# Loads issued earlier, product P1 of the next superblock moved ahead of P3, and the attention's small matmuls put on column tiles

## The chip, the cores and the metric

The kernel runs on one core of a Trainium2 chip. The metric is the device time of one execution in microseconds (us), less being better. TensorE is called PE here as in the profile, VectorE DVE, ScalarE ACT, GpSimd POOL, and SyncE SP; SP issues every DMA of this kernel, in program order.

## The reference

Linear attention with a norm, then two two-layer perceptrons, all float32 (the weights arrive as float64):

```python
kv = np.einsum('bhsd,bhse->bhde', k, v)          # 8 batches, 8 heads, 576 tokens, 64 wide
out = np.einsum('bhsd,bhde->bhse', q, kv)
rms = np.sqrt(np.mean(out * out, axis=-1, keepdims=True) + 1e-06)
x = out / rms * g_norm                           # as 4608 tokens x 512
h = x @ w_in;  x = np.maximum(0.01 * h, h) @ w_out     # 512 -> 2048 -> 512
h = x @ w_in2; x = (h - np.tanh(h)) @ w_out2           # 512 -> 2048 -> 512
```

## The kernel before

**Arithmetic.** Each big product is cut into 2x2 blocks and done with seven block products instead of eight; P1 to P7 are these products (table `PROD`), and `Blocks` adds them up into the four blocks "11", "12", "21", "22". Each float32 operand is split into a high and a low float16 part (`hi` on ACT, `lo` on DVE), and three float16 matmuls make one product (`three`, L489). An operand's splits come as a tile `opa` (for P1, P2, P4) and a tile `ops` (for P3, P5, P6, P7).

**Passes.** There are four in a row: up 1 (`up`, moving operand 288 wide, eight superblocks of eight channel pairs, with the attention of the later batches in between), down 1 (`down`, eight superblocks of two halves t), up 2 and down 2 (256 wide, nine superblocks). An up pass writes its result `g` to DRAM, the next down pass reads it back (`gl`), down 1 writes `x` from tiles `xst`, up 2 reads it as `x1g`. Beside the passes the weights of the next passes are converted from float64 (`convert`: load `words`, ACT L314, four DVE steps, store `wf`) and split (`split_late`: load `unit<-wf`, ACT L362, DVE L365, POOL L372, store `wd`), then loaded into place (`w<-wd`).

**A down superblock.** PE does P1, P2, P4, P6, P7, P5, P3, each over all eight channel pairs j and for both halves. P3 adds on top of P5 in the same PSUM bank `ps_c`, so PE may start P3 of a half only when DVE has read block "22" out of it (`add`, L542). `produce` loads and splits the eight `gl` of the next superblock in the meantime.

**Attention.** For each pair of heads (`pair`): `kv` multiplies k and v of both heads in six float32 matmuls of 128 columns by 128 and uses the two diagonal 64x64 blocks (`kvd`); `qtr` transposes q, `o` multiplies (tile `po`), ACT squares, and `m` sums the squares of each head into row 8r+2c of a 16-row tile `pm`, in one matmul for each half r. In the trace each float32 matmul is two records (two passes). After four pairs, `norms` takes root and inverse (`iv`), stores it, and loads it back spread over the partitions (`bc`, L867), and POOL scales `xg` with it (L874); ACT and DVE then split `xg` (L429, L436).

**Order.** The order on every engine is fixed at build time by `Plan`: each step gets a planned time from the numbers written in the code (`plan.pe` counts PE's time, `chain` places a list of steps on engines A, V and G with their planned durations), and instructions are recorded in that order. A step such as `(None, 4.5, load)` puts the load 4.5 planned us ahead of its first use. At run time engines go through their queues in order and wait on semaphores. Slots L, M and X are buffers handed out by the planner.

Of the kernel before, what the change touches and what calls it, by code (L numbers as in the profile page):

```python
# [130 lines left out]
def body(ctx, tc, q, k, v, g_norm, w1, w2, w3, w4, out):  # L131
# [11 lines left out]
    NU = 4 * P  # L143
    NL, NM, NX = 20, 11, 13

# [23 lines left out]

    ivd = [scratch([2 * H, T1], F32, f"iv_{b}") for b in range(B)]  # L170
    x1d = {(c, s): scratch([P, 2 * T1], F32, f"x1_{c}_{s}") for c in range(DM // P) for s in range(NS1)}
# [20 lines left out]
    mw = const.tile([P, 4, 2 * NP], F32, name="mw")  # L192
    sel = const.tile([P, 4 * H - 2], F32, name="sel")
    kvd = [const.tile([P, P], F32, name=f"kvd{n}") for n in range(2)]

    def constants():
        for h in range(2):
            nc.sync.dma_start(out=gcol[D * h:D * h + D, :], in_=g_norm.rearrange("(p o) -> p o", o=1))
        make_identity(nc, ident)
        nc.vector.memset(ones, 1.0)  # L200
        nc.vector.memset(eps_sb, EPS / (X_SCALE * X_SCALE))
        nc.vector.memset(sel, 0.0)
        for n in range(2):
            nc.vector.memset(sel[D * n:D * n + D, 2 * H - 2 + n:2 * H - 1 + n], 1.0 / D)
            nc.vector.memset(kvd[n], 0.0)
        nc.vector.tensor_reduce(out=gabs, in_=gcol, axis=AX.X, op=ALU.max, apply_absolute_value=True)
# [175 lines left out]
    def split_late(n, i, kk, t, place):  # L382
# [256 lines left out]


    def down(blk, T, NS, mats, width, place, ready, start_of, freed, scales=None, scale=None):

# [32 lines left out]

        def superblock(s):
            t0 = plan.pe
            start_of(s, t0)
            if s + 1 < NS:
                produce(s + 1, t0 + 1.0)  # L680
            dur = mm(width)
            for t in range(2):
                sc = scales(s) if scales else (None, None)
                bk[s, t] = Blocks(
                    dict(a=t, b=2 + 3 * t, c=3 + 3 * t, d=4 + 3 * t), width, place(s, t), None, None, ready(s, t)
                )
                bk[s, t].now = {}
                if scales:
                    def late(s=s, t=t):
                        bk[s, t].scale, bk[s, t].minus = scales(s)  # L690
                    at(t0, late)

            def whole(p, t, js=range(NP)):
# [7 lines left out]
            late = range(len(early), NP)  # L701
            for p in (1, 2):
                for t in range(2):
                    if early:
                        whole(p, t, early)
            for p in (1, 2):
                for t in range(2):
                    whole(p, t, late)
            for j in range(NP):
                for t in range(2):  # L710
                    e = whole(4, t, [j])
                give("A", j, e)
            for p in (6, 7):
                for t in range(2):
                    whole(p, t)
            for t in range(2):
                whole(5, t)
            for t in range(2):
                e = whole(3, t, range(2))
            for j in range(2):  # L720
                give("S", j, e)
                if s == NS - 1:
                    freed(j, e)
            for j in range(2, NP):
                for t in range(2):
                    e = whole(3, t, [j])
                give("S", j, e)
                if s == NS - 1:
                    freed(j, e)

# [13 lines left out]
    PAIRS = (0, 2, 1, 3)  # L744
    D_KV, D_Q, D_O, D_M = 1.6, 0.7, 0.6, 0.55

    def load_pair(b, c, held):
        for nm, src in (("k", k), ("v", v), ("q", q)):
            held[nm] = L.take([CP, NC, 2, D], F32, nm)
            for h in range(2):  # L750
                nc.sync.dma_start(
                    out=held[nm].ap[:, :, h], in_=src[b, 2 * c + h].rearrange("(p c) d -> p c d", p=CP)
                )
# [6 lines left out]
    def pair(b, c, held):  # L760
# [4 lines left out]
        def kv():  # L765
            held["pk"], held["bank"] = att_bank("pk")
            for a in range(NC):
                nc.tensor.matmul(
                    out=held["pk"][:, :P], lhsT=two_heads(held["k"], a), rhs=two_heads(held["v"], a),
                    start=(a == 0), stop=(a == NC - 1),  # L770
                )

        def kv_after(e):
            def go():
                held["kvd"] = kvd[kv_n[0] % 2]
                kv_n[0] += 1
                for h in range(2):
                    r = slice(D * h, D * h + D)
                    nc.scalar.activation(out=held["kvd"][r, r], in_=held["pk"][r, r], func=AF.Copy)
                used.discard(held["bank"])  # L780
# [39 lines left out]

        def m(r):
            first, last = (c == PAIRS[0] and r == 0), (c == PAIRS[-1] and r == 1)
            if first:
                pm[b] = bank(5, "pm")
            row = H * r + 2 * c
            nc.tensor.matmul(
                out=pm[b][:2 * H, :T1], lhsT=sel[:, 2 * H - 2 - row:4 * H - 2 - row], rhs=sq[r].ap,
                start=first, stop=last,
            )
            X.give(sq[r])  # L830

        def m_after(r, e):
            if c == PAIRS[-1] and r == 1:
                norms(b, e)
# [3 lines left out]
            (D_Q, lambda: qtr(1), lambda e: q_after(1, e)), (D_O, lambda: o(0), lambda e: o_after(0, e)),  # L838
            (D_O, lambda: o(1), lambda e: o_after(1, e)), (D_M, lambda: m(0), lambda e: m_after(0, e)),
            (D_M, lambda: m(1), lambda e: m_after(1, e)),  # L840
        ]

    def norms(b, e):
        held = {}

        def root():
            held["iv"] = X.take([2 * H, T1], F32, "iv")
            nc.scalar.activation(
                out=held["iv"].ap, in_=pm[b][:2 * H, :T1], func=AF.Sqrt,
                bias=eps_sb[:2 * H], scale=1.0 / (X_SCALE * X_SCALE),  # L850
            )
# [10 lines left out]
        def load(kk):  # L862
            held[kk] = L.take([P, 4, T1], F32, "bc")
            rows = ivd[b].rearrange("(r h) t -> h r t", r=2)
            for n in range(2):
# [73 lines left out]
    def split_all():  # L939
        for n, (i, kk) in enumerate(UNITS):  # L940
            what = ("w", 0, i - 2, 1) if i >= 2 else "s_w1"
            when(what, plan.now + 0.3 + 2.5 * n, lambda i=i, kk=kk: plan.chain(plan.now, split_first(i, kk)))

    scaled[0] = [split_all]

    def early_pair(b, c, t, held):
        gaps = (0.0, 1.7, 2.5, 3.4, 4.4, 5.2, 6.2)
        for (dur, fn, after), g_ in zip(pair(b, c, held), gaps):
# [61 lines left out]

    spread(lambda i, kk, t: convert(1, i, kk, t, 6.0), UNITS, START + 52.0, START + 180.0)
    spread(lambda i, kk, t: split_late(1, i, kk, t, M), UNITS, START + 200.0, end1 - 60.0)
    spread(lambda i, kk, t: convert(2, i, kk, t, 6.0), UNITS, START + 182.0, end1 - 60.0)

# [80 lines left out]
    def x1_operands(s, t):  # L1095

        x1ops[s] = [{}, {}]
        for kk in range(2):
# [64 lines left out]
    c3 = end2 + 0.45 * (end3 - end2)  # L1163
    spread(lambda i, kk, t: convert(3, i, kk, t, 6.0), UNITS, end2 - 45.0, c3)
    e = c3 + 18.0
    scaled[3] = [lambda: [down_scales(state[x]) for x in ("whole", "rest")]]
    spread(lambda i, kk, t: split_late(3, i, kk, t, M), UNITS, e + 1.0, end3 - 55.0)


# [71 lines left out]
```

## Time and profile before

| | |
|---|---|
| median of 3 runs | 1646.12 us (1645.23 to 1646.91) |
| profiled execution | 1649.15 us, of which the span from first to last instruction is 1647.4 us |
| PE busy | 1512.3 us, 92% |
| DVE, ACT, POOL busy | 79%, 53%, 45% |
| granted PE clock, mean | 0.959 |

The profile is of one execution. The stages can be told apart in it: preparation and the first attention to 105 us, up 1 to 602, down 1 to 942, up 2 to 1309, down 2 to the end. A matmul's end is modelled and overlaps the next one's start, so what PE has done is read from start to start.

### The profile page before, as it was taken

How to read it: one execution, taken by the hardware profiler on the slowest of the kernel's cores; microseconds unless marked ns; L12 is line 12 of the kernel's file. 1: busy time of each engine (PE TensorE's matmuls, PEld its weight loads, DVE VectorE, ACT ScalarE, POOL GpSimd, SP SyncE). 2: the span in 40 equal slices, each digit the busy share in tenths (PEclk: the TensorE clock that was granted, in tenths of full speed). 3: DMA queues.
4: the chain of work that ended last, by engine and by line, in shares of the span. 5: the costliest groups of instructions: out<-in, count | busy, mean ns of one | idle time of the engine just before them, and what ended most of it. 6: DMA issues, size and time to landing. Idle time of an engine off the chain costs nothing. (4 is left out here: it accounts for less than half of the span.)

```text
span 1647.4 us, 32120 instructions
## 1 busy us (share of the span) xinstructions
PE 1512.3 (92%) x12274; PEld 1227.4 (75%) x12274; DVE 1301.6 (79%) x2113; ACT 867.2 (53%) x1381; POOL 746.0 (45%) x758
## 2 busy tenths in 40 slices
PE   5299898898989999999999979999999889999998
PEld 3156675666767777777777768888888778888887
DVE  4765676576667778889989669999999988888881
ACT  3366454465655664444444246666776645455441
POOL 0356203144143345666656134446887654444440
PEclk8589999999999999999999989999999999999999
DMA  9856897898896885545455565555666844444441
GB/s 210 172 88 160 227 239 208 245 245 235 252 259 209 282 318 168 185 145 200 155 172 173 184 233 206 186 210 196 243 240 243 316 143 143 157 129 135 145 132 33
DMA packets 251578, 322.08 MB, mean 196 GB/s; under 512 B 129440, under 2 KB 194080, under 8 KB 251424
## 3 DMA queue, kind: packets, MB, share of 16 engines
q1 hardware_dynamic: 251424, 320.03, 62.7%
q8 instruction: 96, 1.57, 0.4%
q14 instruction: 58, 0.48, 0.1%
HBM read 190.84 MB, written 129.12 MB: 194 GB/s over the span
## 5 line engine op out<-in xcount | busy, mean ns | idle before, releaser
L489 PEld LDWEIGHTS <-w 128*128 128x128 f16 x8400 | 824.8, 99 | 280.1 <-issue 98.7
L468 POOL TENSOR_TENSOR gl<-gl 128x256 f32<-128x256 f32 (+1 forms) x272 | 309.5, 1138 | 307.2 <-issue 79.9
L489 PE MATMUL ps_c<-ops,w 128*128 128x288 f16 (+1 forms) x2400 | 337.3, 285 | 40.2 <-DVE g L536 28.2
L489 PE MATMUL ps_a<-ops,w 128*128 128x288 f16 (+1 forms) x2400 | 333.6, 284 | 22.2 <-ACT u L527 10.3
L489 PEld LDWEIGHTS <-ops 128*128 128x128 f16 x1728 | 169.8, 98 | 28.8 <-issue 7.7
L372 POOL TENSOR_TENSOR unit<-unit 128x128 f32<-128x128 f32 x192 | 134.1, 699 | 116.0 <-DVE wo L365 97.4
L489 PE MATMUL ps_b<-opa,w 128*128 128x288 f16 (+1 forms) x1200 | 170.2, 287 | 0.0
L489 PE MATMUL ps_a<-opa,w 128*128 128x288 f16 (+1 forms) x1200 | 166.8, 283 | 2.9 <-DMA w<-wd 2.8
L489 PE MATMUL ps_d<-opa,w 128*128 128x288 f16 (+1 forms) x1200 | 165.9, 282 | 2.7 <-DVE g L536 2.7
L468 DVE TENSOR_TENSOR gl<-gl 128x256 f32<-128x256 f32 (+1 forms) x272 | 156.0, 576 | 3.3
L874 POOL TENSOR_TENSOR xg<-xg,bc 128x1152 f32<-128x1152 f32 x16 | 43.1, 2694 | 254.3 <-DMA bc<-iv 208.7
L1145 POOL TENSOR_TENSOR g<-g,th 128x512 f32<-128x512 f32 x72 | 101.0, 1403 | 95.9 <-ACT th L1142 95.7
L431 ACT ACTIVATE ops<-gl,inv 128x1024 f16<-128x1024 f32 x72 | 82.6, 1147 | 110.2 <-POOL gl L468 102.9
L489 PEld LDWEIGHTS <-opa 128*128 128x128 f16 x1296 | 126.8, 98 | 16.6 <-issue 1.9
L429 ACT ACTIVATE ops<-gl 128x1152 f16<-128x1152 f32 x64 | 74.3, 1162 | 99.5 <-POOL gl L468 94.6
L438 DVE SCALAR_TENSOR_TENSOR ops<-gl,inv,ops 128x1024 f16<-128x1024 f32 x72 | 104.4, 1451 | 15.8 <-ACT ops L431 15.4
L436 DVE TENSOR_TENSOR ops<-gl,ops 128x1152 f16<-128x1152 f32 x64 | 99.8, 1559 | 19.9 <-ACT ops L429 19.7
L365 DVE SCALAR_TENSOR_TENSOR wo<-unit,s_w,wo 128x384 f16<-128x384 f32 (+1 forms) x96 | 83.4, 871 | 27.1 <-ACT wo L362 26.7
L489 PE MATMUL ps_c<-w,ops 128*128 128x256 f16 x864 | 98.4, 275 | 3.8 <-DVE osb L536 3.8
L489 PE MATMUL ps_a<-w,ops 128*128 128x256 f16 x864 | 96.1, 273 | 3.2 <-ACT u L527 3.2
L468 POOL TENSOR_TENSOR x1g<-x1g 128x256 f32<-128x256 f32 x72 | 68.1, 946 | 65.1 <-DMA x1g<-x 34.7
L438 DVE SCALAR_TENSOR_TENSOR opa<-gl,inv,opa 128x768 f16<-128x768 f32 x72 | 87.2, 1211 | 12.5 <-ACT opa L431 12.5
(118 smaller groups left out, 2192.3 us busy)
## 6 DMA issues: line engine op xcount, KB each, us to landing
g<-g SPq DMA_DIRECT2D x64, 576.0 KB, 4.4
gl<-g SPq DMA_DIRECT2D x64, 576.0 KB, 4.7
g<-g SPq DMA_DIRECT2D x72, 512.0 KB, 3.0
gl<-g SPq DMA_DIRECT2D x72, 512.0 KB, 4.5
wd<-wo SPq DMA_DIRECT2D x48, 448.0 KB, 2.8
w<-wd SPq DMA_DIRECT2D x24, 896.0 KB, 7.4
words<-in_moe_w_in_dram SPq DMA_DIRECT2D x64, 256.0 KB, 5.0
words<-in_moe_w_out_dram SPq DMA_DIRECT2D x64, 256.0 KB, 4.0
```

The costliest lines, as they stand in the source:

```text
L365: nc.vector.scalar_tensor_tensor(out=dst()[:, 1, a:b], in0=cols(0, n), scalar=scale(), in1=dst()[:, 0, a:b], op0=ALU.mult, op1=ALU.subtract,)
L372: nc.gpsimd.tensor_tensor(out=o, in0=a, in1=b, op=ALU.subtract)
L429: nc.scalar.activation(out=o, in_=i_, func=AF.Copy)
L431: nc.scalar.activation(out=o, in_=i_, func=AF.Identity, scale=scale())
L436: nc.vector.tensor_tensor(out=o, in0=i_, in1=h, op=ALU.subtract)
L438: nc.vector.scalar_tensor_tensor(out=o, in0=i_, scalar=scale(), in1=h, op0=ALU.mult, op1=ALU.subtract)
L468: lambda: e.tensor_tensor(out=g()[:, o], in0=g()[:, a], in1=g()[:, b], op=op),
L489: nc.tensor.matmul(out=out_, lhsT=a, rhs=c, start=start and m == 0, stop=stop and m == n - 1, skip_group_check=not fresh,)
L874: nc.gpsimd.tensor_tensor(out=x, in0=x, in1=held[kk].ap, op=ALU.mult)
L1145: e.tensor_tensor(out=g()[:, n], in0=g()[:, n], in1=held["t"].ap[:, n], op=ALU.subtract)
```

## The change

- Leads of loads: `words` 6 to 13 planned us, `unit` 4.5 to 9, `bc` 5 to 6, `x1g` 5 to 10 with the whole chain begun 13 us earlier (15 for the first), q, k and v of later batches 13 instead of 9 places ahead. Slots: L 20 to 22, X 13 to 8.
- `down`: P1 of superblock s+1 is done between P5 and P3 of superblock s, pair by pair; P2 and P4 alternate pair by pair. `produce` starts 6.8 planned us before P2 (`AHEAD`), where it started 1 us after the start of P1.
- `kv`: each head gets matmuls of its own, 64 columns by 64, in two column tiles of PE's array (`tile_position` (0, 0) and (0, 64)); k and v lie with each head's rows together, so a DMA row is 384 elements instead of six times 64. `m`: one 32-column tile for each half, both halves issued together. `iv` has 64 rows instead of 16.
- Planned PE durations of a pair: 1.6, 0.7, 0.7, 0.6, 0.6, 0.55, 0.55 become 0.9, 0.5, 0.5, 0.6, 0.6, 0.7. The first weights are split unit pair by unit pair.

```diff
-    NL, NM, NX = 20, 11, 13
+    Q = 32
+    NL, NM, NX = 22, 11, 8
...
-        plan.chain(t, [(None, 4.5, load), (None, 0.0, room)] + stages + [(None, 0.0, store)])
+        plan.chain(t, [(None, 9.0, load), (None, 0.0, room)] + stages + [(None, 0.0, store)])
...
+    AHEAD = 6.8
...
-            if s + 1 < NS:
-                produce(s + 1, t0 + 1.0)
...
-            early = range(NP - 2) if s == 0 else range(0)
...
+            def in_turn(ps, s=s, then=None):
+                for j in range(NP):
+                    for p in ps:
+                        for t in range(2):
+                            e = whole(p, t, [j], s)
+                    if then:
+                        then(j, e)
+
+            start_of(s, plan.pe)
+            if s == 0:
+                blocks(0)
+                for js in (range(NP - 2), range(NP - 2, NP)):
+                    for p in (1, 2):
+                        for t in range(2):
+                            whole(p, t, js)
+            if s + 1 < NS:
+                produce(s + 1, plan.pe - AHEAD - (one if s == 0 else 0.0))
+            in_turn((4,) if s == 0 else (2, 4), then=lambda j, e: give("A", j, e))
+            for p in (6, 7, 5):
                 for t in range(2):
                     whole(p, t)
+            if s + 1 < NS:
+                blocks(s + 1)
+                in_turn((1,), s + 1)
...
+            in_turn((3,), then=end)
...
-    D_KV, D_Q, D_O, D_M = 1.6, 0.7, 0.6, 0.55
+    D_KV, D_Q, D_O, D_M = 0.9, 0.5, 0.6, 0.7
...
+            apart = nm != "q"
+            held[nm] = L.take([CP, 2, NC, D] if apart else [CP, NC, 2, D], F32, nm)
...
-                nc.tensor.matmul(
-                    out=held["pk"][:, :P], lhsT=two_heads(held["k"], a), rhs=two_heads(held["v"], a),
-                    start=(a == 0), stop=(a == NC - 1),
-                )
+                for h in range(2):
+                    nc.tensor.matmul(
+                        out=held["pk"][D * h:D * h + D, :D], lhsT=held["k"].ap[:, h, a], rhs=held["v"].ap[:, h, a],
+                        start=(a == 0), stop=(a == NC - 1), tile_position=(0, D * h), skip_group_check=True,
+                    )
...
+            for r in range(2):
+                nc.tensor.matmul(
+                    out=pm[b][Q * r:Q * r + Q, :T1], lhsT=sel[:, Q - 2 - 2 * c:2 * Q - 2 - 2 * c], rhs=sq[r].ap,
+                    start=first, stop=last, tile_position=(0, Q * r), skip_group_check=True,
+                )
+                X.give(sq[r])
...
-            more.append([(None, 5.0, lambda kk=kk: load(kk)), ("G", 2.7, lambda kk=kk: scale(kk))] + stages)
+            more.append([(None, 6.0, lambda kk=kk: load(kk)), ("G", 2.7, lambda kk=kk: scale(kk))] + stages)
...
-    OFFS = (1, 4, 6, 8, 10, 12, 14)
+    OFFS = (1, 4, 6, 8, 10, 13)
...
-            loads.append((n0 - 9, b, c, held))
+            loads.append((n0 - 13, b, c, held))
...
-    spread(lambda i, kk, t: convert(1, i, kk, t, 6.0), UNITS, START + 52.0, START + 180.0)
+    spread(lambda i, kk, t: convert(1, i, kk, t, 13.0), UNITS, START + 45.0, START + 173.0)
...
-            plan.chain(t + 3.5 * kk, [(None, 5.0, load)] + stages)
+            plan.chain(t + 3.5 * kk, [(None, 10.0, load)] + stages)
...
-            state["whole"] = second_scales(0, whole, t0 + 9.0)
-            x1_operands(0, t0 + 17.0)
+            state["whole"] = second_scales(0, whole, t0 + 5.0)
+            x1_operands(0, t0 + 2.0)
...
-            x1_operands(n // (NOP * NP) + 1, plan.pe + 1.0)
+            x1_operands(n // (NOP * NP) + 1, plan.pe - 12.0)
```

On PE at the start of up 1, where a pair's `kv` and `m` stand between two float16 products (before, then now):

```order
L489 LDWEIGHTS w_0_688
L489 MATMUL ps_b<-opa,w_0_688 128x288
L768 MATMUL pk<-v,k 128x128 x6
L826 MATMUL pm<-sq,sel 16x288
L489 LDWEIGHTS w_0_688
L489 MATMUL ps_a<-ops,w_0_688 128x288
```

```order
L490 LDWEIGHTS w_0_712
L490 MATMUL ps_b<-opa,w_0_712 128x288
L832 MATMUL pm<-sq,sel 32x288 x2
L774 MATMUL pk<-v,k 64x64 x12
L490 LDWEIGHTS w_0_712
L490 MATMUL ps_a<-ops,w_0_712 128x288
```

Six matmuls of `kv` become twelve of a quarter of the area, and the two of `m` stand next to each other instead of apart.

On SP in the middle of up 1, where the inverse norms of a batch (`iv_74`) are stored and loaded back (before, then now):

```order
L751 DMA q<-in_q_dram 96x6x64 x2
L859 DMA iv_74<-iv 16x288
L867 DMA bc<-iv_74 64x2x288 x4
L606 DMA g_3_7_140<-g 128x1152
L390 DMA unit<-wf_2_1_250 128x512
L867 DMA bc<-iv_74 64x2x288 x4
L347 DMA wf_2_1_266<-unit 128x512
L302 DMA words<-in_moe_w_in_dram 128x2x256 x2
```

```order
L756 DMA q<-in_q_dram 96x6x64 x2
L303 DMA words<-in_moe_w_in_dram 128x2x256 x2
L864 DMA iv_74<-iv 64x288
L398 DMA wd_0_293<-wo 128x1792
L872 DMA bc<-iv_74 64x2x288 x4
L607 DMA g_3_7_140<-g 128x1152
L391 DMA unit<-wf_2_0_249 128x512
L872 DMA bc<-iv_74 64x2x288 x4
```

The store and the two sets of `bc` keep their places to each other; the `words` load has moved ahead of them, and a `unit` load still stands between the sets.

On SP at the end of down 1, where the weights of up 2 (`w`) and the operands of its second superblock (`x1g`, which reads `x_0_1` and others) are loaded (before, then now):

```order
L415 DMA w_5_10838<-wd_5_306 128x3584
L415 DMA w_6_10846<-wd_6_307 128x3584
L415 DMA w_7_10873<-wd_7_308 128x3584
L1111 DMA x1g<-x_0_0_77 128x64
L1111 DMA x1g<-x_0_1_78 128x448
L1111 DMA x1g<-x_2_0_93 128x64
```

```order
L1120 DMA x1g<-x_3_0_101 128x64
L1120 DMA x1g<-x_3_1_102 128x448
L1044 DMA x_2_7_100<-xst 128x288
L416 DMA w_0_10992<-wd_0_301 128x3584
L416 DMA w_1_11001<-wd_1_302 128x3584
```

The eight `x1g` loads of the second superblock stood behind all eight `w` loads and now stand ahead of them.

## Rows read from the trace of the kernel before

**Rows 1.** Busy time by stage; columns: stretch, length, busy us by engine, clock, DMA, GB/s.

```profile
0.00:105.00 105.00, 54.02 (x206) 35.20 (x207) 66.52 (x137) 39.93 (x84) 30.86 (x46) 0.69 0.81 168
105.00:602.00 497.00, 459.37 (x3399) 340.05 (x3398) 333.55 (x642) 281.78 (x535) 161.09 (x185) 0.96 0.80 234
602.00:942.00 340.00, 327.16 (x2616) 257.97 (x2616) 299.79 (x427) 154.05 (x201) 195.60 (x184) 0.98 0.52 172
942.00:1309.00 367.00, 346.25 (x3103) 304.72 (x3104) 338.41 (x579) 238.78 (x379) 219.73 (x215) 0.98 0.65 231
1309.00:1648.00 339.00, 325.52 (x2954) 289.43 (x2951) 263.37 (x333) 152.69 (x184) 138.71 (x130) 0.99 0.42 132
```

**Rows 2.** ACT's waits in up 1: us in total, times, longest us.

```profile
ACT wo L362 <- DMA unit<-wf: 22.4, 3, 8.8
ACT opa L429 <- POOL xg L874: 14.3, 10, 3.5
ACT unit L314 <- DMA words<-in_moe_w_out_dram: 13.6, 3, 8.2
```

**Rows 3.** Timeline of all engines in up 1: start us, us, engine, line, operation.

```profile
449.05 0.37 SPq L859 DMA_DIRECT2D iv<-iv  x1
452.94 2.59 SPq L867 DMA_DIRECT2D bc<-iv  x4
455.57 0.59 SPq L390 DMA_DIRECT2D unit<-wf  x1
...
460.53 0.61 ACT L362 ACTIVATE wo<-unit,s_w 128x384 f16<-128x384 f32 x1 [8.77 <-DMA unit<-wf]
...
461.49 0.90 PE L489 MATMUL ps_a<-ops,w 128*128 128x288 f16 x6 [3.85 <-ACT u L525]
```

**Rows 4.** Timeline of PE in up 1, around a pair's small matmuls.

```profile
117.12 0.65 PE L804 MATMUL po<-qt,kvd 128*128 128x288 f32 x2
117.61 0.90 PE L489 MATMUL ps_a<-opa,w 128*128 128x288 f16 x6
...
122.67 1.50 PE L768 MATMUL pk<-v,k 96*128 96x128 f32 x12
124.01 0.90 PE L489 MATMUL ps_d<-opa,w 128*128 128x288 f16 x6
...
137.93 0.90 PE L489 MATMUL ps_a<-ops,w 128*128 128x288 f16 x6
138.76 0.66 PE L826 MATMUL pm<-sq,sel 128*16 128x288 f32 x2
139.35 0.91 PE L489 MATMUL ps_c<-ops,w 128*128 128x288 f16 x6
```

**Rows 5.** DMA in up 1: packets by size, and issues with KB each and us to landing.

```profile
DMA packets 128308, 116.45 MB, mean 234 GB/s; under 512 B 86038, under 2 KB 109702, under 8 KB 128263
...
g<-g SPq DMA_DIRECT2D x63, 576.0 KB, 4.4
...
k<-in_k_dram SPq DMA_DIRECT2D x46, 144.0 KB, 4.6
```

**Rows 6.** Timeline of all engines at the start of up 2.

```profile
938.52 3.85 SPq L415 DMA_DIRECT2D w<-wd  x6
...
960.48 0.93 ACT L431 ACTIVATE opa<-x1g,s_x 128x768 f16<-128x768 f32 x1 [12.82 <-DMA x1g<-x]
...
961.83 1.44 PE L489 MATMUL ps_a<-ops,w 128*128 128x256 f16 x6 [10.33 <-ACT u L527]
```

**Rows 7.** PE's waits in down 1: us in total, times, longest us.

```profile
PE ps_c L489 <- DVE xst L542: 11.9, 8, 2.8
```

**Rows 8.** Timeline of all engines in down 1, at a change of superblock.

```profile
898.10 1.05 DVE L436 TENSOR_TENSOR opa<-gl,opa 128x864 f16<-128x864 f32 x1
899.36 6.04 PE L489 MATMUL ps_a<-opa,w 128*128 128x288 f16 x48
...
905.24 1.02 PE L489 MATMUL ps_b<-opa,w 128*128 128x288 f16 x7
```

More of the change, by code (lines that the diff above doesn't have):

```diff
@@ L168, in scratch @@
         return dram.tile(shape, dt, tag=name, name=name)
-    ivd = [scratch([2 * H, T1], F32, f"iv_{b}") for b in range(B)]
+    ivd = [scratch([2 * Q, T1], F32, f"iv_{b}") for b in range(B)]
     x1d = {(c, s): scratch([P, 2 * T1], F32, f"x1_{c}_{s}") for c in range(DM // P) for s in range(NS1)}
@@ L192, in body @@
     mw = const.tile([P, 4, 2 * NP], F32, name="mw")
-    sel = const.tile([P, 4 * H - 2], F32, name="sel")
+    sel = const.tile([P, 2 * Q - 2], F32, name="sel")
     kvd = [const.tile([P, P], F32, name=f"kvd{n}") for n in range(2)]
@@ L203, in constants @@
         for n in range(2):
-            nc.vector.memset(sel[D * n:D * n + D, 2 * H - 2 + n:2 * H - 1 + n], 1.0 / D)
+            nc.vector.memset(sel[D * n:D * n + D, Q - 2 + n:Q - 1 + n], 1.0 / D)
             nc.vector.memset(kvd[n], 0.0)
@@ L674, in work_, with blocks @@
             return plan.on_pe(3 * len(js) * dur, go)
-        def superblock(s):
-            t0 = plan.pe
-            start_of(s, t0)
-            if s + 1 < NS:
-                produce(s + 1, t0 + 1.0)
-            dur = mm(width)
+        dur = mm(width)
+        one = 2 * NP * 3 * dur
+        def blocks(s):
             for t in range(2):
-                sc = scales(s) if scales else (None, None)
                 bk[s, t] = Blocks(
@@ L690, in late, with superblock, whole @@
                         bk[s, t].scale, bk[s, t].minus = scales(s)
-                    at(t0, late)
-            def whole(p, t, js=range(NP)):
+                    at(plan.pe, late)
+        def superblock(s):
+            def whole(p, t, js=range(NP), s=s):
                 e = work_(s, p, t, js, dur)
@@ L698, in give, with end @@
                 at(e, lambda: (M if kind == "A" else L).give(ops[s, j][kind]))
-            early = range(NP - 2) if s == 0 else range(0)
[L701 to L713, printed above, removed]
+            def in_turn(ps, s=s, then=None):
[16 more added lines that the diff above has]
+            for p in (6, 7, 5):
                 for t in range(2):
                     whole(p, t)
[L716 to L720, printed above, removed]
+            if s + 1 < NS:
+                blocks(s + 1)
+                in_turn((1,), s + 1)
+            def end(j, e):
                 give("S", j, e)
@@ L723, in superblock @@
                     freed(j, e)
[L724 to L729, printed above, removed]
+            in_turn((3,), then=end)
         return produce, superblock, span
@@ L744, in body @@
     PAIRS = (0, 2, 1, 3)
-    D_KV, D_Q, D_O, D_M = 1.6, 0.7, 0.6, 0.55
+    D_KV, D_Q, D_O, D_M = 0.9, 0.5, 0.6, 0.7
     def load_pair(b, c, held):
         for nm, src in (("k", k), ("v", v), ("q", q)):
-            held[nm] = L.take([CP, NC, 2, D], F32, nm)
+            apart = nm != "q"
+            held[nm] = L.take([CP, 2, NC, D] if apart else [CP, NC, 2, D], F32, nm)
             for h in range(2):
                 nc.sync.dma_start(
-                    out=held[nm].ap[:, :, h], in_=src[b, 2 * c + h].rearrange("(p c) d -> p c d", p=CP)
+                    out=held[nm].ap[:, h] if apart else held[nm].ap[:, :, h], in_=src[b, 2 * c + h].rearrange("(p c) d -> p c d", p=CP)
                 )
@@ L778, in go @@
                     r = slice(D * h, D * h + D)
-                    nc.scalar.activation(out=held["kvd"][r, r], in_=held["pk"][r, r], func=AF.Copy)
+                    nc.scalar.activation(out=held["kvd"][r, r], in_=held["pk"][r, :D], func=AF.Copy)
                 used.discard(held["bank"])
@@ L819, in o_after, with m, m_after @@
             plan.do("V", end, 0.46, copy)
-        def m(r):
-            first, last = (c == PAIRS[0] and r == 0), (c == PAIRS[-1] and r == 1)
+        def m():
+            first, last = c == PAIRS[0], c == PAIRS[-1]
             if first:
                 pm[b] = bank(5, "pm")
[L825 to L833, printed above, removed]
+            for r in range(2):
[4 more added lines that the diff above has]
+                X.give(sq[r])
+        def m_after(e):
+            if c == PAIRS[-1]:
                 norms(b, e)
@@ L846, in root @@
         def root():
-            held["iv"] = X.take([2 * H, T1], F32, "iv")
+            held["iv"] = X.take([2 * Q, T1], F32, "iv")
             nc.scalar.activation(
-                out=held["iv"].ap, in_=pm[b][:2 * H, :T1], func=AF.Sqrt,
-                bias=eps_sb[:2 * H], scale=1.0 / (X_SCALE * X_SCALE),
+                out=held["iv"].ap, in_=pm[b][:2 * Q, :T1], func=AF.Sqrt,
+                bias=eps_sb[:2 * Q], scale=1.0 / (X_SCALE * X_SCALE),
             )
@@ L863, in load @@
             held[kk] = L.take([P, 4, T1], F32, "bc")
-            rows = ivd[b].rearrange("(r h) t -> h r t", r=2)
+            rows = ivd[b].rearrange("(r q) t -> q r t", r=2)
             for n in range(2):
@@ L939, in split_all, with pair_ @@
     def split_all():
-        for n, (i, kk) in enumerate(UNITS):
+        def pair_(i):
+            for kk in range(2):
+                plan.chain(plan.now + 2.5 * kk, split_first(i, kk))
+        for i in range(NP):
             what = ("w", 0, i - 2, 1) if i >= 2 else "s_w1"
-            when(what, plan.now + 0.3 + 2.5 * n, lambda i=i, kk=kk: plan.chain(plan.now, split_first(i, kk)))
+            when(what, plan.now + 0.3 + 5.0 * i, lambda i=i: pair_(i))
     scaled[0] = [split_all]
     def early_pair(b, c, t, held):
-        gaps = (0.0, 1.7, 2.5, 3.4, 4.4, 5.2, 6.2)
+        gaps = (0.0, 1.2, 2.0, 2.9, 3.9, 5.7)
         for (dur, fn, after), g_ in zip(pair(b, c, held), gaps):
```

11 lines of the change are left out of this document (5 added, 6 removed).

## The prediction, made before the run

> **What bounds the kernel now.** The busy time by stage comes first [rows 1]. From 105 us on, PE is busy 92 to 96% of every stage, so a stage ends when PE has done its products, and what PE idles or runs at half clock is what can be won there. Up 1 has most of it: 497.0 - 459.4 = 37.6 us idle and a granted clock of 0.96; down 1 has 12.8 us, up 2 20.8 and down 2 13.5. In the first 105 us PE is busy for 54.0 only and the DMA engines for 81%: preparation waits for data.
>
> Next, who makes PE wait in up 1. ACT stands still for late loads: 22.4 us for `unit`, 13.6 for `words` and 14.3 for `xg`, which POOL scales once `bc` has landed [rows 2]. One case in order of time shows the chain [rows 3]. SP stores `iv` at 449.05 and can issue `bc` only at 452.94, when the store has landed; behind four `bc` the `unit` load goes out at 455.57. ACT waits 8.77 us for it until 460.53, with the evacuation of `ps_a` behind it in its queue, and so PE waits 3.85. PE thus swallows about 4.9 us of an ACT wait and pays the rest. This comes back with each batch of the attention.
>
> **Late loads in up 1.** The lead of `unit` grows by 4.5 planned us. The load still stands between two `bc` sets in SP's queue, but an ACT wait of 8.77 becomes one of 4.3, under the 4.9 that PE swallows. `words` gets 7 us more, against a longest wait of 8.2. `bc` gets 1 us more, against a longest wait of 3.5, and its way (store, landing, four issues, landing) stays, so this part is largely left. By shares, (22.4 + 13.6) / 50.3 = 72% of 37.6 us, 27 us, belongs to loads that now come in time and 10.6 to `bc`. I take **-25**; the ends are -12 (half of the first part) and -34.
>
> The clock: 4% of 497 us, times PE's share of 0.92, is 18 us of work lost at 1.2 GHz. The low stretches follow waits: behind the one at the start of up 2 six matmuls of 256 columns take 1.44 us [rows 6], where six of 288 take 0.90 in a stretch without a wait [rows 4]. If it shrinks as the waits do, 25/37.6 of it goes, 12 us; I take **-10**, ends -5 and -17.
>
> **kv.** Now twelve passes take 124.01 - 122.67 = 1.34 us, 0.112 each for 128 moving columns [rows 4]. A pass of `po` takes (117.61 - 117.12) / 2 = 0.245 for 288 [rows 4], so a pass costs its moving columns, whatever its weights. The change makes 24 passes of 64 columns, 0.056 each, on two tiles of the array. If the tiles run side by side that is 0.67 us, if not 1.34. A form that uses a part of the columns also pays at its edges, as `pm` with 16 columns shows: six float16 matmuls take 5.88 / 8 = 0.735 us from start to start [rows 8], but `pm` begins 0.83 after the six ahead of it, and it ends 0.59 after its start where `po` needs 0.49 [rows 4]: 0.095 + 0.10 = 0.195 us in all. So `kv` will take 0.87 or 1.53. Of the eight batches six lie in up 1, 24 pairs: 24 x (0.87 - 1.34) = -11.3, or +4.6. I take **-11**, because time goes by streamed columns here and two tiles stream into different columns.
>
> The row shows loads of weights hidden under passes: twelve in a row at 0.112, none left over [rows 4]. The Trainium skill, page "TensorE: Matmul & The Clock Gate", section "Part 3: Packing small matmuls — row/col tiling", says that a weight load overlaps matmuls in flight only if it goes to another row group. Column tiles share theirs, so by the rule each of the 24 passes would first show its load; by it the sum ends at 1611, by the row at 1563. The rule read to the letter would have shown these loads in the trace too, and it does not.
>
> **m.** Two matmuls apart cost 2 x (0.195 + 0.49) = 1.37 us a pair. Side by side they pay the edges once, and the four passes of 0.245 take 0.49 (all overlap) to 0.98 (none). Two passes of one tile must follow each other and a third can only join the second, so I take 0.735: 0.93 in all, 24 x 0.44 = **-11**, ends -16 and -5.
>
> **Down 1.** All of PE's waits in it, eight of 11.9 us, are P3's for DVE to have emptied `ps_c` [rows 7]. P1 of the next superblock, 5.88 us for both halves [rows 8], now lies between; the longest wait is 2.8, so it covers all, and DVE's queue is the cover: without it P3 waits as before. With 2% of 340 us at half clock, of which I let 3 go, that is -15. Against it: P1 needs the eighth `opa` earlier. In the profile DVE ends it at 899.15 and PE reaches it at 899.36 + 7/8 x 2.94 = 901.93, 2.8 us later [rows 8]. Counted from the end of P5, PE used to reach the eighth pair after P3's 5.88 us and 2.57 of P1, 8.5 in all; now it does after 7/8 x 5.88 = 5.1, so 3.4 earlier. Production moves up by 1.9 (from 4.9 to 6.8 before P2): 1.5 are lost and 1.3 left. DVE is busy 88% here, so some superblocks will miss it; I allow +3, ends 0 and +10. Together **-12**.
>
> **Up 2.** Its start has the longest stall: `x1g` was issued behind six `w` loads, ACT waited 12.82 us and PE 10.33 [rows 6]. The loads now stand ahead of `w` and the chain begins 13 us earlier: all of it goes, with about 2 of half clock: **-12**, ends -6 and -13. The other half of the 20.8 us stays: DVE is busy 338.4 of 367 us, and no work of it is removed.
>
> **The rest.** Down 2's first superblock loses its wait of P3; I take **-3** of 13.5 idle, ends 0 and -6. Preparation: k at 144 KB lands in 4.6 us while `g` with four times the bytes takes 4.4, and 86038 of 128308 packets in up 1 are under 512 B [rows 5]; k and v now go in rows of 1536 B, 18 of the 64 loads of each ahead of up 1. Loads of two batches share a stage that also waits for conversions: **-3**, ends 0 and -8. Fewer X slots and earlier loads can bring waits for a slot. None stands in the rows; a third of a us in each of the 34 superblocks would be 11. I allow **+4**, ends 0 and +11.
>
> **Sum.** -25 - 10 - 11 - 11 - 12 - 12 - 3 - 3 + 4 = -83. The profiled execution took 1649.15 us, 3.0 above the median of the runs, so 1646.12 - 83 = **1563 us**.
>
> **Rivals.** (a) The tiles do not run side by side: `kv` +5 where I have -11, `m` -5 where I have -11, so 1563 + 22 = 1585. For it: no row shows two tiles at once. (b) As (a) for `kv`, and every load of weights shows, as long as its pass: 24 x 0.112 + 0.195 = 2.88 us instead of 0.87, 24 x 2.0 = 48 more, 1611. The page quoted above stands for it. (c) The loads stay late, since SP still waits for the `iv` store in front of them and more is in flight: half of the first two terms, 1580. For it: DMA is 80% busy in up 1. (d) The operands of P1 come too late. P1 now blocks PE's queue with P3 behind it, and the 15 changes of superblock in the down passes pay each time: it decides from 83 / 15 = 5.5 us each, that is if `opa` ends 6.8 us later than now. With 6 us each the time is 1653. Against it: 1.3 us of margin are left by the rows, and DVE would need 300 of 328 us. (e) That the change does nothing would need the leads not to reach SP's queue; the order printed above shows that they do.
>
> **Chances and range.** Forecast 0.53, (a) 0.20, (b) 0.05, (c) 0.17, (d) 0.05. About 0.2% is what a measurement can tell here. Only (d) reaches before: slower 0.04, same 0.01, faster 0.95. The lower bound takes the far ends of late loads, clock, `m`, preparation and slots for a good part: 1563 - 27 = 1536. The upper takes (a) and (c) together, 1602, and a little for the slots: 1607.
>
> **What would show it.** Up 1 should last 435 to 445 us with PE idle for under 15; `kv` 0.85 to 0.9 us from its start to the next product, `m` 0.9; no waits of `ps_c` on `xst` in down 1; no PE wait over 3 us at the start of up 2; under 40000 packets below 512 B in up 1. A `kv` of 1.5 says (a), of 2.9 (b); waits of ACT for `unit` or `words` over 5 us say (c); waits of P1 on `opa` in each superblock say (d). Wrong altogether would be a clock below 0.95 in up 1, or a stage where DVE is busy throughout and PE waits for it.

## The result, and the profile after

| | before | after |
|---|---|---|
| median of the runs | 1646.51 us (1645.23 to 1648.07) | 1582.32 us (1579.08 to 1584.01) |
| profiled execution, its span | 1649.15, 1647.4 us | 1581.95, 1580.1 us |
| ratio, 95% interval | | 0.9607 (0.9590 to 0.9625) |

The kernel is faster by 64.2 us; the forecast was 83 (1563 us, with 1536 to 1607 as its range). To see where the two differ, both traces are cut at the first product of each stage; for the kernel before that is at 105.3, 590.0, 942.0 and 1301.1 us, so up 1 and up 2 end 12 and 8 us ahead of the planned bounds of [rows 1], and the last column ends with the last matmul. The lengths, in us:

| | preparation | up 1 | down 1 | up 2 | down 2 |
|---|---|---|---|---|---|
| before | 105.3 | 484.7 | 352.0 | 359.1 | 341.8 |
| after | 101.6 | 435.5 | 341.4 | 360.3 | 336.9 |
| difference | -3.7 | -49.2 | -10.6 | +1.2 | -4.9 |
| forecast | -3 | -57 | -12 | -12 | -3 |

Each length is of one execution. In seven of the kernels below, the changed one among them, up 1 is the same, and it lasts 433.1 to 438.2 us; so differences of up to 5 us between stage lengths carry no reading alone.

The busy time of up 1 and up 2 in the kernel after (stretch, length, then busy us of PE, PEld, DVE, ACT and POOL, the granted clock, the DMA share and GB/s):

```profile
101.60:537.10 435.50, 414.81 (x3611) 312.25 (x3610) 324.60 (x633) 274.99 (x527) 162.47 (x181) 0.99 0.80 256
878.50:1238.90 360.40, 337.88 (x3033) 296.96 (x3031) 334.47 (x574) 235.11 (x377) 210.67 (x210) 0.99 0.64 228
```

and the same view of the kernel before, at the new cuts:

```profile
105.30:590.00 484.70, 449.67 (x3323) 332.66 (x3322) 326.62 (x635) 275.03 (x529) 157.29 (x183) 0.96 0.80 231
942.00:1301.10 359.10, 338.36 (x3030) 297.65 (x3031) 330.51 (x572) 234.91 (x376) 212.19 (x210) 0.98 0.65 230
```

In up 1 PE's idle time goes from 35.0 us to 20.7 and its busy time from 449.7 to 414.8. In up 2 PE is idle for 22.5 us, where before it was 20.7: the largest miss. DVE stands beside it, busy for 334.5 of 360.4 us.

The small matmuls of the attention, on PE's timeline (start us, us, operation; to be held against [rows 4]):

```profile
114.76 0.65 PE L490 MATMUL ps_c<-ops,w 128*128 128x288 f16 x4
115.34 0.68 PE L832 MATMUL pm<-sq,sel 128*32 128x288 f32 x4
115.95 0.91 PE L490 MATMUL ps_b<-opa,w 128*128 128x288 f16 x6
116.70 0.90 PE L490 MATMUL ps_a<-ops,w 128*128 128x288 f16 x6
117.53 0.92 PE L774 MATMUL pk<-v,k 96*64 96x64 f32 x24
118.38 0.91 PE L490 MATMUL ps_d<-opa,w 128*128 128x288 f16 x6
```

From its start to the next product `kv` takes 0.85 us and both parts of `m` together 0.61; with the 0.095 us ahead of each (117.53 - 116.70 = 0.83 for six products that take 0.735) that is 0.945 instead of 1.34, and 0.705 instead of 1.37. So `kv` gives 24 x 0.395 = 9.5 us and `m` 24 x 0.665 = 16, 25.4 in all. The weight loads of this `kv` (ns: shortest, median, longest):

```profile
L774 PEld LDWEIGHTS pk<-v,k x24: 133/138/138, 117.5 to 118.2; 96*64 96x64 f32 x24
```

What ACT, PE and SP wait for in up 1 (us in total, times, longest us; of ACT the longest rows on POOL or DMA, to be held against [rows 2]):

```profile
ACT opa L430 <- POOL xg L879: 18.2, 8, 5.1
...
ACT wo L363 <- POOL unit L373: 3.9, 3, 2.3
ACT sq L816 <- DMA iv<-iv: 2.9, 1, 2.9
```

```profile
PE ps_c L490 <- DVE g L537: 10.1, 9, 2.2
PE po L810 <- ACT qt L802: 5.8, 2, 4.0
```

```profile
SPq L872 <- DMA iv<-iv: 14.6, 6, 4.8
```

ACT no longer waits for a load of `unit` or `words`; what it waits for is `xg`, more than before (18.2 us against 14.3). New is a wait of 2.9 us of `sq` for the `iv` store: both take slots X, of which there are 8 now instead of 13. One case of `xg`, on the timeline of SP's queue and then of the engines behind it:

```profile
396.50 0.57 SPq L864 DMA_DIRECT2D iv<-iv  x1
400.03 2.56 SPq L872 DMA_DIRECT2D bc<-iv  x4
402.69 0.60 SPq L607 DMA_DIRECT2D g<-g  x1
403.40 0.38 SPq L391 DMA_DIRECT2D unit<-wf  x1
403.87 1.03 SPq L398 DMA_DIRECT2D wd<-wo  x1
404.94 2.02 SPq L303 DMA_DIRECT2D words<-in_moe_w_in_dram  x2
407.01 2.59 SPq L872 DMA_DIRECT2D bc<-iv  x4
...
413.27 2.61 POOL L879 TENSOR_TENSOR xg<-xg,bc 128x1152 f32<-128x1152 f32 x1 [4.94 <-DMA wf<-unit]
...
415.92 0.92 ACT L430 ACTIVATE opa<-xg 128x864 f16<-128x864 f32 x1 [5.08 <-POOL xg L879]
...
416.75 0.39 ACT L802 ACTIVATE qt<-pq 128x288 f32<-128x288 f32 x1
...
417.19 0.85 PE L810 MATMUL po<-qt,kvd 128*128 128x288 f32 x1 [4.03 <-ACT qt L802]
```

The first four `bc` wait for the `iv` store, the second four stand behind five other issues, the last of them goes out at 409.0, and a `bc` here needs 3.3 to 4.8 us to land; POOL scales at 413.27 (the profile puts the wait down to a `wf` store that went out at 409.70, but POOL's instruction reads `xg` and `bc` alone, and the last `bc` is due 3.3 to 4.8 us after 409.0), ACT has stood for 5.08 us, `qt` is behind it in ACT's queue, and PE pays 4.03. It is the mechanism of [rows 3], with another load at its end.

In down 1 the waits of `ps_c` for `xst` [rows 7] are gone but for one of 0.2 us, and P1 waits for `opa` 2.6 us in all. PE's waits in up 2:

```profile
PE ps_c L490 <- DVE g L537: 16.7, 24, 2.2
PE ps_a L490 <- ACT u L528: 2.5, 1, 2.5
PE pt L223 <- DVE m_w L259: 1.7, 1, 1.7
PE pt L223 <- DVE mx L1068: 1.1, 1, 1.1
```

The stall of 10.33 us [rows 6] is gone. In its place PE waits 16.7 us for DVE in pieces of up to 2.2, where before it was 9.7 us in 21.

### The profile page after: what moved, and what is told of

Same layout as the page of the kernel before. It is cut to its first block, busy times and chain, and to the rows that moved or that the text cites. A ratio compares the mean times of both kernels' runs of the same rounds, so it can differ in the third digit from the quotient of the medians.

```text
span 1580.1 us, 33070 instructions
## 1 busy us (share of the span) xinstructions
PE 1468.2 (93%) x12658; PEld 1197.5 (76%) x12658; DVE 1311.1 (83%) x2113; ACT 864.4 (55%) x1381; POOL 749.4 (47%) x758
## 5 line engine op out<-in xcount | busy, mean ns | idle before, releaser
L490 PE MATMUL ps_c<-ops,w 128*128 128x288 f16 (+1 forms) x2400 | 331.7, 282 | 27.0 <-DVE g L537 26.8
L490 PE MATMUL ps_b<-opa,w 128*128 128x288 f16 (+1 forms) x1200 | 174.7, 283 | 0.0
L490 PE MATMUL ps_d<-opa,w 128*128 128x288 f16 (+1 forms) x1200 | 173.0, 281 | 0.6 <-DVE g L537 0.5
L469 DVE TENSOR_TENSOR gl<-gl 128x256 f32<-128x256 f32 (+1 forms) x272 | 161.9, 601 | 3.7
L528 ACT ACTIVATE u<-ps_a,up 128x256 f32<-128x256 f32 x144 | 68.2, 473 | 49.2 <-PE ps_a L490 43.8
L537 DVE SCALAR_TENSOR_TENSOR g<-ps_c,u 128x288 f32<-128x288 f32 x128 | 57.7, 451 | 39.2 <-PE ps_c L490 39.1
```

Source lines behind the costliest of these rows:

```text
L469: lambda: e.tensor_tensor(out=g()[:, o], in0=g()[:, a], in1=g()[:, b], op=op),
L490: nc.tensor.matmul(out=out_, lhsT=a, rhs=c, start=start and m == 0, stop=stop and m == n - 1, skip_group_check=not fresh,)
L528: nc.scalar.activation(out=t, in_=src, func=AF.Identity, scale=self.scale)
L537: nc.vector.scalar_tensor_tensor(out=o, in0=src, scalar=self.minus if sub else self.scale, in1=t, op0=ALU.mult, op1=ALU.add,)
```

## The experiments

Times are medians; ratios are to runs of the kernel before on the same chip; differences in us are to the median of the changed kernel where nothing else is said, and stage lengths, clocks and waits are of the profiled execution. First come the parts of the change, alone on the kernel before or undone in the changed one, then what binds up 2 and up 1 in the changed kernel.

**Column tiles alone**, on the kernel before:

```
-            for a in range(NC):
-                nc.tensor.matmul(out=pk[:, :P], lhsT=two_heads(k, a), rhs=two_heads(v, a), ...)
+            for a in range(NC):
+                for h in range(2):
+                    nc.tensor.matmul(out=pk[D*h:D*h+D, :D], lhsT=k.ap[:, a, h], rhs=v.ap[:, a, h],
+                                     ..., tile_position=(0, D*h))
```

and `m` as in the change, with the planned durations that go with them. 

> The kernel before with the column tiles of kv and m alone (k and v keep their layout, all leads stay). In the changed kernel kv came to the next product 0.395 us earlier and m 0.665 earlier, 24 of each in up 1. Theory: up 1 is bound by what PE issues, so the saving goes to the end: 24 x 1.06 = 25 us, 1621 us, with PE's idle time in up 1 still near 35. Rival: up 1 runs at the pace of its late loads, and quicker products only wait longer for them: 1638 or more, with PE's idle time at 45 or more.

1614.75 us, ratio 0.9814 (0.9785 to 0.9842). Up 1 lasts 457.4 us, 27.3 less, and PE idles in it for 36.2, as before:

```profile
103.10:560.50 457.40, 421.19 (x3612) 314.25 (x3611) 323.33 (x631) 272.62 (x525) 158.80 (x176) 0.97 0.82 246
```

So time saved in PE's small products goes to the end, and the rival falls. Of the other 6 us 2.2 lie in preparation, which has the small products of two batches, and 3.7 in down 1, which this edit doesn't touch.

**Leads alone**, on the kernel before (`convert(..., 13.0)`, `unit` 9.0, `bc` 6.0, `n0 - 13`, as in the change; the slots L, M and X are 21, 12 and 10, and the two halves of a first weight are split as one chain). 

> The kernel before with the leads of words, unit, bc, k, v and q of the changed kernel and nothing else of its order (the slots are shared out anew for it, 21, 12 and 10, and the two halves of a w1 unit start as one chain). The prediction's terms for late loads and half clock would give -35: 1613 us. Theory now: in the changed kernel taking the leads back cost only 13 us, because the chain from the iv store over bc to xg stays and goes on stopping ACT when unit and words no longer do: -13 to -18, 1630 to 1636 us, with ACT waits for unit and words gone and those for xg at 14 us or more.

1620.77 us, ratio 0.9843 (0.9811 to 0.9874): 27 us, between the two. Up 1 is 23.4 us shorter: 15.0 of them idle time (35.0 to 20.0), 8.5 busy time at a granted clock of 0.98 instead of 0.96. ACT's waits for `unit` and `words` are gone as expected, and those for `xg` nearly double:

```profile
ACT opa L429 <- POOL xg L874: 26.8, 10, 4.9
```

**Leads put back** in the changed kernel. 

> The changed kernel with the leads of words, unit, k, v, q and bc as they were before. Theory: the late unit and words loads come back, PE's idle time in up 1 goes from 20.7 to about 35 us and the granted clock from 0.99 to 0.97, so 1605 us (20 to 28 more). Rival: the loads came in time because SP's queue and the DMA engines have less to do (k and v in longer rows, a shorter attention): then within 5 us of the changed kernel, and no ACT waits for unit over 3 us.

1595.13 us, ratio 0.9681 (0.9659 to 0.9703): +13 us, less than expected and more than the rival gives, which also falls by ACT's waits in up 1:

```profile
ACT unit L315 <- DMA words<-in_moe_w_in_dram: 16.4, 5, 8.1
...
ACT wo L363 <- DMA unit<-wf: 9.4, 3, 4.2
```

Up 1 lasts 451.6 us, 16.1 more: 8.5 of idle time (29.2 against 20.7) and 7.6 of busy time, at a granted clock of 0.97 instead of 0.99. The leads are thus worth 27 us alone and 13 beside the rest of the change.

**k and v in the old layout** (`apart = False`), the rest as changed. 

> The changed kernel with k and v as two heads side by side again, in rows of 256 B; column tiles, leads and order stay. Theory (the prediction's term): preparation loses 3 us and up 1 nearly nothing, 1585 us, although packets under 512 B in up 1 go from 32000 to over 70000. Rival: the longer rows are what brings the other loads in time: 1595 us or more, with ACT waits for unit or words in up 1.

1587.98 us, ratio 0.9642 (0.9624 to 0.9661): +5.7 us. Up 1 lasts 440.1 us, 4.6 more, preparation 101.2, no more. Packets under 512 B in up 1 are back at 82382 (31695 in the changed kernel), a load of `k` lands in 5.6 us where it takes 4.3 in the changed kernel, and ACT waits longer for `xg`:

```profile
ACT opa L430 <- POOL xg L879: 26.1, 10, 5.1
```

So the layout seems to have its worth not where the forecast put it, in preparation, but in up 1, by way of `xg`. How is not shown: a `bc` lands in 3.7 us against 3.6, and 440.1 us is just outside the 433.1 to 438.2 that the same up 1 takes.

**The old order of the superblocks** in the down passes, the rest as changed. 

> The changed kernel with the order of the superblocks in the down passes as before (P1 of the next superblock after P3, not between P5 and P3). Theory: P3's waits for ps_c come back, about 12 us in down 1 and 5 in down 2 with some half clock: 1597 us (1593 to 1601). Rival: other parts of the change (slots, leads) made the waits vanish: within 4 us of the changed kernel, no PE waits for ps_c over 1 us in down 1.

1591.73 us, ratio 0.9645 (0.9615 to 0.9675): +9.4 us, a little less than expected. Down 1 lasts 350.1 us (+8.7) and down 2 340.3 (+3.4). The waits are back, nearly as in [rows 7]:

```profile
PE ps_c L490 <- DVE xst L543: 11.6, 6, 2.9
```

**The chain of x1g as late as before**, the rest as changed:

```
-            state["whole"] = second_scales(0, whole, t0 + 5.0)
-            x1_operands(0, t0 + 2.0)
+            state["whole"] = second_scales(0, whole, t0 + 9.0)
+            x1_operands(0, t0 + 17.0)
```

with the load's lead at 5.0 and `plan.pe + 1.0` in `between2`. 

> The changed kernel with the chain of x1g (its load, its start in the last superblock of down 1, its start in up 2) as late as before. Theory A: DVE's work binds up 2, so the stall of some 10 us at its start comes back, the small PE waits for DVE in ps_c fall from 16.7 to about 10, and the time is within 4 us of the changed kernel (1578 to 1586). Rival B: the small waits come from something else that the change did to the order, they stay at 15 or more, and the stall is paid: 1590 to 1594.

1581.85 us, ratio 0.9601 (0.9581 to 0.9622): no change against 0.9607 (0.9590 to 0.9625). Up 2, and PE's waits around and in it:

```profile
878.50:1241.50 363.00, 338.76 (x3031) 297.36 (x3032) 334.45 (x575) 234.57 (x377) 211.52 (x211) 0.98 0.65 229
```

```profile
PE ps_c L490 <- DVE g L537: 12.7, 23, 1.9
PE ps_a L490 <- ACT u L528: 11.2, 1, 11.2
```

The stall is back with 11.2 us instead of 2.5, and the time stays. All waits for DVE together (`g`, `m_w` and `mx`) fall from 19.5 to 12.7 us and so pay 6.8 of the 8.7; those for `g` fall to 12.7 and not to 10. The profiled execution alone is less exact than the median: up 2 is 2.7 us longer in it and down 1 4.9, while its preparation is 4.5 shorter.

**DVE's half of tanh's subtraction left out**, so two of the four blocks of `g` are not subtracted from; POOL's half stays. 

> The changed kernel without DVE's half of the subtraction of tanh in up 2 (two of four blocks of g keep their value; POOL's half stays): 67 x 1.088 = 73 us of DVE's 335 in up 2 go. Theory A, DVE's work binds up 2: PE's waits for ps_c there all but vanish, its 22 us of idle time fall to about 9 as in down 1, and the time is 1568 us (1564 to 1572). Rival B, the waits come from where DVE's work stands, or from loads: up 2 keeps at least 18 us of idle time and the time stays within 4 us of the changed kernel.

1565.26 us, ratio 0.9480 (0.9450 to 0.9510): -17 us. Up 2 lasts 344.8 us, and PE's waits for `g` in `ps_c` fall to 2.5:

```profile
876.20:1221.00 344.80, 335.54 (x3031) 297.60 (x3031) 268.60 (x507) 233.08 (x375) 195.24 (x210) 0.99 0.67 236
```

**Three of its four blocks on POOL**:

```
-            [("V", 0.65, lambda: two(nc.vector, slice(0, 2))), ("G", 1.5, lambda: two(nc.gpsimd, slice(2, 4)))],
+            [("V", 0.35, lambda: two(nc.vector, slice(0, 1))), ("G", 2.2, lambda: two(nc.gpsimd, slice(1, 4)))],
```

> The changed kernel with three of the four blocks of that subtraction on POOL and one on DVE (the same result). DVE loses 67 x 0.54 = 36 us in up 2, POOL gains about 47 and goes from 211 to some 258 of 360 us. Theory A: half of the gain of leaving out all of DVE's half, 1575 us (1571 to 1579). Rival: POOL's slower part makes g late or slows DVE's other instructions, which run beside it: 1582 or more.

1591.10 us, ratio 0.9643 (0.9609 to 0.9677): slower by 9, as the rival has it. DVE's busy time in up 2 rises to 343.4 us, although it has half the columns to subtract, and PE waits 22.0 us in `ps_c`. The subtraction on the two engines (busy us, mean ns):

```profile
L1154 POOL TENSOR_TENSOR g<-g,th 128x768 f32<-128x768 f32 x68 | 128.7, 1894 | 81.1 <-ACT th L1151 78.6 <-DMA x1g<-x 2.2 <-DMA g<-g 0.3
...
L1154 DVE TENSOR_TENSOR g<-g,th 128x256 f32<-128x256 f32 x67 | 63.2, 944 | 3.5 <-ACT th L1151 3.5
...
L439 DVE SCALAR_TENSOR_TENSOR ops<-x1g,s_x,ops 128x512 f16<-128x512 f32 x32 | 36.0, 1137 | 0.0
```

In the changed kernel the same rows are

```profile
L1154 POOL TENSOR_TENSOR g<-g,th 128x512 f32<-128x512 f32 x68 | 93.9, 1382 | 94.5 <-ACT th L1151 94.0 <-DMA g<-g 0.6
L1154 DVE TENSOR_TENSOR g<-g,th 128x512 f32<-128x512 f32 x67 | 72.8, 1088 | 4.3 <-ACT th L1151 4.3
...
L439 DVE SCALAR_TENSOR_TENSOR ops<-x1g,s_x,ops 128x512 f16<-128x512 f32 x32 | 33.7, 1066 | 0.0
```

Half the columns take DVE 87% of the time. That led to the opposite edit.

**The whole subtraction on DVE**, `("V", 0.65, lambda: two(nc.vector, slice(0, 4)))` and nothing on POOL. 

> The changed kernel with the whole subtraction of tanh in up 2 on DVE (128x1024 in one instruction) and none on POOL. With three blocks on POOL, DVE's one block of 256 columns took 944 ns, and its two blocks of 512 take 1088, so its time there is hardly one of columns. Theory: it is mostly waiting while POOL's instruction runs beside it; alone it goes at about 1 ns a column as DVE's other float32 work on 512 columns does (0.53 to 0.68 us), so 1024 columns take 1.07 us, DVE's busy time in up 2 stays at 330 us or falls, and the time is 1578 us (1572 to 1584). Rival: the time goes by columns at the 2.1 ns that the trace shows, 2.18 us each: 73 us more DVE work in up 2 and about 1630 us.

1567.77 us, ratio 0.9514 (0.9481 to 0.9548): -15 us, more than expected. Up 2 lasts 347.7 us, and DVE is busy for 319.3, 15 less with twice the columns; PE waits 7.7 us for `g`:

```profile
880.90:1228.60 347.70, 334.86 (x3033) 296.19 (x3031) 319.25 (x573) 233.04 (x375) 125.82 (x142) 1.00 0.66 234
```

```profile
L1154 DVE TENSOR_TENSOR g<-g,th 128x1024 f32<-128x1024 f32 x67 | 87.0, 1301 | 3.9 <-ACT th L1151 3.9
...
L439 DVE SCALAR_TENSOR_TENSOR ops<-x1g,s_x,ops 128x512 f16<-128x512 f32 x32 | 24.9, 792 | 0.0
```

**The same with the chain of x1g late**, which tells whether the stall was free because of DVE. 

> The changed kernel with the whole subtraction on DVE (as in the run where up 2 fell to 347.7 us) and the chain of x1g as late as before the change. Theory A: the stall at the start of up 2 cost nothing in the changed kernel only because DVE set the stage's length; with PE waiting for DVE less, most of the stall of some 11 us is now paid: up 2 at 354 to 358 us and 1574 to 1578 us. Rival: PE's queue or the buffers make up for the stall whoever sets the pace: within 3 us of 1568.

1576.73 us, ratio 0.9578 (0.9554 to 0.9602): 9 us more than with the chain early, and up 2 lasts 358.0 us instead of 347.7.

```profile
875.60:1233.60 358.00, 337.51 (x3032) 297.42 (x3032) 320.95 (x574) 233.94 (x376) 128.53 (x142) 0.98 0.65 231
```

```profile
PE ps_a L490 <- ACT u L528: 11.5, 1, 11.5
PE ps_c L490 <- DVE g L537: 6.2, 10, 1.6
```

The same stall that cost nothing where DVE set the pace now costs 9 us. Of the 9.4 us by which that wait grows, the waits for DVE pay 3.3 (9.5 in the run before, 1.8 of it for `mx`), so there is little left to pay it from. DVE's busy share doesn't tell the two cases apart (93% of up 2 in the changed kernel, 92% in the run before this); how long PE waits for DVE does.

**The load of bc planned 10 us ahead** instead of 6, for all batches but the first. 

> The changed kernel with the load of bc planned 10 us ahead of the scaling instead of 6, for every batch but the first. Of PE's 20.7 us of idle time in up 1 some 15 follow the chain from the iv store over bc to xg. Theory: the plan asks for the operands too close behind bc, so with 4 us more the ACT waits for xg (18.2 us) go to below 6 and PE gains about 10: 1572 us. Rival: the plan starts the chain from the iv store, so 4 us more only move all that follows to 4 us later, and the operands are late for the product instead: 1582 us or more.

1574.07 us, ratio 0.9539 (0.9511 to 0.9567): -8 us. ACT waits for `xg` 1.2 us in all, and up 1 lasts 427.8 us with 15.7 idle:

```profile
99.80:527.60 427.80, 412.14 (x3612) 311.43 (x3611) 335.17 (x633) 276.99 (x527) 159.89 (x180) 0.99 0.81 261
```

```profile
ACT opa L430 <- DMA wf<-unit: 8.5, 2, 7.1
ACT sq L816 <- DMA iv<-iv: 6.9, 2, 4.8
```

```profile
PE pm L832 <- ACT sq L816: 2.5, 1, 2.5
```

The next late arrivals show at once: the split of `xg` now waits 8.5 us for a `wf` store (both use slots M), and `sq` 6.9 for the `iv` store (slots X), of which PE pays 2.5.

**Both edits**, `bc` 10 us ahead and the whole subtraction on DVE, on the changed kernel. 

> The changed kernel with bc planned 10 us ahead (up 1 then 427.8 us instead of 435.5) and the whole subtraction of tanh on DVE (up 2 then 347.7 instead of 360.3). Theory: the two act in different stages and add up: 7.7 + 12.6 = 20 us under the changed kernel, 1561 us (1556 to 1566). Rival: what is won in up 1 or up 2 is given back at the next stage, whose loads of w are then late: 1568 or more.

1559.55 us (1557.96 to 1565.02), ratio 0.9467 (0.9445 to 0.9490): 23 us under the changed kernel. Up 2 lasts 348.0 us and up 1 432.4; whether `bc` gives less here than alone (427.8) one execution doesn't tell, and the medians add up (8 and 15). It is the fastest of the kernels here.

## Why the prediction was right or wrong, step by step

**What bounds the kernel.** That a stage ends when PE has done its products held for up 1, down 1 and down 2, and failed for up 2. The prediction had the number (DVE busy 338.4 of 367 us) and used it only to say that the other half of the idle time stays. It should have said that the stage goes by DVE's work: a stall of PE at its start is time that PE otherwise spends waiting for DVE later.

**Up 2, -12: +1.2 came.** This is the step that failed. The mechanism was right as far as it went (the stall is gone), but the time came back as waits for DVE in `ps_c`. Three runs show it: the stall put back costs nothing that the medians show, DVE's work taken out shortens the stage by 15.5 us, and with DVE's load lighter the same stall costs 9. The last line of the forecast named the sign, a stage where DVE is busy throughout and PE waits for it, as what would make it wrong altogether; it made one term wrong.

**Late loads, -25: -14.3 came** (idle time in up 1, 35.0 to 20.7), and -15.0 with the leads alone. `unit` and `words` came in time, as argued. The mis-sized term is the share: ACT's waits were taken to share out PE's idle time, 72% to the loads that are mended and 28% to `bc`. Yet when the loads no longer stop ACT, the next arrival in the same batch, `xg`, does: its waits grew from 14.3 to 18.2 us, and to 26.8 with the leads alone. The run with `bc` earlier took 8 us of that. So rival (c), which put the time at 1580, was nearest by number, and its reason (SP still waits for the `iv` store) holds for `bc`; its sign, ACT waits for `unit` or `words` of over 5 us, did not come. Nor did PE's idle time in up 1 of under 15 us: it is 20.7. That up 1 lasts 435.5 us, inside the 435 to 445 that were named, is luck of the bounds: the forecast took 57 from 497.0, up to the planned bound, and by the first products up 1 had 484.7 and lost 49.

**The clock, -10:** PE's busy time in up 1 fell by 34.9 us, 25.4 of them in the attention, so 9.4; the granted clock there is 0.99 instead of 0.96.

**kv, -11: -9.5.** Two tiles run side by side; a `kv` costs 0.945 us where 0.87 was worked out. **m, -11: -16**, the far end: the four passes took no more than two would, so the third and fourth joined the first two. Rival (a) falls by both. So does (b): with it the 24 loads of weights, which are 133 to 138 ns each in the rows of `pk`, would have stood one behind the other, over 3 us; all 24 and their passes fit in 0.85. That goes against the rule of the Trainium skill, "TensorE: Matmul & The Clock Gate", section "Part 3: Packing small matmuls — row/col tiling", that a load overlaps matmuls in flight only when its row group differs: here both tiles have the same rows. (The same section also lets a load go ahead into a background weight buffer; no run here tells whether that is what happens.)

**Down 1, -12: -10.6,** and +8.7 with the old order put back. The waits for `xst` went, and P1's for `opa` cost 2.6 us, where 3 was allowed. Rival (d) falls. **Down 2, -3: -4.9;** the old order costs 3.4.

**Preparation, -3: -3.7,** but not for the reason given. In the changed kernel and the runs above it lasted 97.1 to 103.1 us, whatever was changed, so a term of this size can't be read there; the layout of `k` and `v` showed itself, if anywhere, in up 1, with 4.6 us. **Slots, +4:** no run tests it by itself, but the wait was there to see: ACT's `sq` waits for the `iv` store in every run with 8 slots X, 1.3 to 8.3 us in all, and in none with 10 or 13. In the changed kernel it is 2.9 us, and no row has PE waiting behind it.

**The sum** in the profiled executions is -67.2 us (1649.15 to 1581.95), 16 less than 83: up 2 lacks 13 and the late loads 11, `m` gives 5 more and the 4 allowed for the slots are not seen, the rest is under 2 each. So the range held although one term of nine came to nothing and another to little more than half. The other 3 us are the base: the profiled execution before was 3.0 above its median, and the one after is not.

The parts give 33 (tiles) and 27 us (leads) alone on the kernel before, 9 (order of the superblocks) and 6 (layout) undone in the changed one: 75 for a change that gives 64. They overlap in up 1, as the leads show: with the rest of the change in place they are worth half. Why tiles alone gave 33 us rather than the 25 of their products in up 1 stays open.

## What to carry to other kernels

Before a stall of one engine is booked as a gain, look whom that engine waits for in the rest of the stage: here a stall cost nothing while another engine set the pace, and its time came back as many small waits. Waits of one queue are not shares of a loss: with the first mended, the next late arrival took a good part of its place here, so follow the chain to what remains late. And moving work to an idle engine can slow the busy one; try the other direction too.

## What the runs showed of the hardware

Two column tiles of the array work at the same time, for float32 too: `m` with two tiles and four passes of 0.245 us takes 0.61 us to the next product, and `kv` with 24 passes takes 0.85.

DVE's subtraction of two SBUF tensors takes 944 ns for 256 columns beside a POOL instruction of 1894, 1088 for 512 beside one of 1382, and 1301 for 1024 with none of them beside it. DVE's split of `x1g` on 512 columns, which also reads two SBUF tensors, goes from 1137 to 1066 to 792 ns in the same three kernels. The evacuations of `ps_c`, with one input in PSUM, stay at 473, 473 and 474 ns. One by one the changed kernel's rows of up 2 show more. Where none of POOL's subtractions runs beside it, DVE's of 512 columns takes 0.68 us at its shortest. Where POOL's begins first and overlaps it, DVE's ends 0.54 to 0.56 us after POOL's in 23 of 26 pairs, as here at 1009.64 against 1009.10:

```profile
1007.83 1.27 POOL L1154 TENSOR_TENSOR g<-g,th 128x512 f32<-128x512 f32 x1 [1.86 <-ACT th L1151]
1008.04 1.60 DVE L1154 TENSOR_TENSOR g<-g,th 128x512 f32<-128x512 f32 x1
```

So DVE's stands until POOL's is done. The Trainium skill, page "SBUF — State Buffer", section "Who interferes with whom", says that a DVE instruction with two SBUF inputs contends with a GpSimd instruction that reads SBUF, and that the ports they share are an exclusive lock; these rows agree with it. That DVE's time in such an instruction counts as busy in the profile is the trap: 334 busy us of 360 looked like work, and 15 of them went away when DVE was given more.
